# An attention and two-layer kernel on one core: planner latencies, due times, PSUM rings and two half-width chunks changed

## The chip, the cores and the metric

The kernel runs on one core of a Trainium2 chip. The metric is device time in microseconds (us) of one execution. Before the change the median of three runs is 897.53 us (896.87 to 906.74).

## The reference, cut to what matters

```python
def phi(x):                                   # x: (4, 8, 576, 64), omega: (128, 64)
    proj = einsum('bhsd,md->bhsm', x, omega)
    h = proj - sum(x * x, axis=-1, keepdims=True) / 2
    h = h - max(h, axis=-1, keepdims=True)
    return exp(h) / sqrt(m)
q_p, k_p = phi(q * D**-0.25), phi(k * D**-0.25)
kv, z = einsum('bhsm,bhsd->bhmd', k_p, v), sum(k_p, axis=2)
attn = einsum('bhsm,bhmd->bhsd', q_p, kv) / (einsum('bhsm,bhm->bhs', q_p, z)[..., None] + 1e-06)
x = attn.transpose(0, 2, 1, 3).reshape(2304, 512)
x = softplus(x @ w_in) @ w_out                # 512 -> 2048 -> 512
x = silu(x @ w_in2) @ w_out2                  # 512 -> 2048 -> 512, float32 out
```

The weights arrive as float64 bits and are turned into float32 on the chip.

## The kernel before, in words

Every large product is done on pairs of reduced-precision numbers: a float32 operand is split into a high part (a cast on ScalarE) and a low part (`diff`, a subtraction on VectorE), and three matmuls replace one. The program has four stages on TensorE, in this order.

**Attention with the first product of layer 1.** There are five token blocks: four of 512 tokens (one batch each) and one of 256 (the four tails). `attention(b)` works in pieces, each a half of the heads of 256 tokens. A piece of k is *projection* (16 matmuls into two PSUM tiles), *exponential* on ScalarE, and the *kv* product. A piece of q is projection and exponential, and then twice (e = 0, 1): *flip* (four transposes into `pq`), a copy `qt` by ScalarE, *num* (by the halves of the array, into `pn`), a division on VectorE (`den`, `xn`), and *back* (two transposes into `px`). When both backs are there, ScalarE writes the high part of x and VectorE the low part. The square term of phi enters in one of two ways. With the "fold", ScalarE squares the transposed input and 16 further matmuls by `neg_half` (L577) add it to the projection; VectorE then takes one maximum (L590). Without it, a second copy of the input lies in natural order, ScalarE squares that, and VectorE makes a row sum (`sums`, L548), the maximum (L592) and two small shifts (L600, L601). Before the change the k and q pieces of batch 0 and the k tail of batches 0 and 1 use the fold (`n < 2`, `bp == 0`, `sb == 0`). `first_layer(sb)` multiplies block sb by 16 chunks of 128 columns of w_in: 12 matmuls of up to 512 columns (L819 to L821), a copy to `g` (L825) and a store to DRAM (L829). The attention of block sb + 1 is woven between the chunks of block sb.

**Second product of layer 1**, **first product of layer 2**, **second product of layer 2.** These use seven block products in place of eight (the order 1, 5, 6, 2, 7, 3, 4). Their weights are prepared in pairs of row blocks by `sums_of`: a load `raw` (L353), a scaling by ScalarE (L358), three steps on VectorE (L362, L367, L372), then casts and sums, and stores to a DRAM buffer `ws` (L460), eight pairs for each of three matrices. Pairs of the first two matrices are prepared during the first stage, those of the last during layer 2's first product. `load_w` (L1070) brings sets of block weights back from `ws`. `load_b` (L863) brings back the stored activations `gate`, softplus runs on them (L867), `combine` and `split` (L874, L889, L279) make the operands `g`, and the products are L941 and L947. Layer 2's first product is L1191; between its products ScalarE copies PSUM banks away (`snap`, L1201) and VectorE adds to them (L1206).

**What sets the order.** `Order` (L88 to L260) collects items, each with an engine, a time that it occupies the engine, a lag until its result can be used, the tiles that it takes, and a due time. A list scheduler then simulates the four queues with these numbers and writes out, for every engine, one fixed sequence; of the items that could start it takes the one due first. On the chip each engine goes through its own sequence in order and waits by semaphores. The numbers of the planner have no effect on the chip other than by this sequence. Of these numbers the change touches among others: the lag of ScalarE, the transfer model (`RATE` bytes per us, `ARRIVE` us), the slack that a due time gets (`WAIT`, `AHEAD`), how far ahead weights are fetched (`FETCH`, `EARLIER`), and the due time of each weight pair (`PREP`). PSUM has two rings of four banks, `bank` and `y`; `PLACE` says which of them kv, flip, num and back use, and the projections of batch 0 use `y`.

Of the kernel before, what the change touches and what calls it, by code (L numbers as in the profile page):

```python
# [18 lines left out]
P = 128  # L19
T = 256  # L20
# [29 lines left out]
STAY = 5.39  # L50
GT, TURN = 0.18, 0.1
# [9 lines left out]
BACKLOG, SOON = 1.0, 6.6  # L61
EARLIER = 23.24
AHEAD, WAIT = 2.88, 2
RATE = 380e3
ARRIVE = 2.0
ISSUE = 0.5
BEGIN = 36.0
SHARE = (2.2, 1.3, 1.75, 0.45, 0.0)
PREP = tuple(140.0 + 11.1 * n for n in range(8)) + tuple(237.9 + 12.7 * n for n in range(8)) + tuple(542.0 + 14.0 * n for n in range(8))
# [6 lines left out]
def on_act(n, psum=False):  # L76
    return ((0.04 if psum else 0.10) + n / 1193, 0.15)
# [183 lines left out]
def attention_moe_moe_kernel(  # L261
# [79 lines left out]
    def unpack(layer, fc, io, raw_tag, into, tf, first, after, due=None):  # L341
# [34 lines left out]
        b = add("ACT", (0.575, 0.15), scale, [a], alloc=[tf] if opens else [], uses=[traw] + ([] if opens else [tf]))  # L376
# [116 lines left out]
    def inputs(s, name, xT, xN, vs, fold, held, after):  # L493
# [31 lines left out]
        for i, (v, shape) in enumerate(vs or ()):  # L525
# [3 lines left out]
            def load_v(i=i, v=v, shape=shape, opens=opens):  # L529
                if tw is None:  # L530
                    x = get("ld", [P, VW], F32, f"v_{name}_{i}")
                else:
                    if opens:
                        s["both"] = get("wb", [P, 2 * VW], F32, f"v_{name}")
                    x = s["all"][:, XW:] if tw is here else s["both"][:, i * VW : (i + 1) * VW]
# [22 lines left out]
    def features(s, name, simple, fold, ins, cols, sq_of, psums):  # L558
# [6 lines left out]
        tps = [new(psums) for _ in range(2)]  # L565
# [74 lines left out]

    def main_cols():
        return [0, P, T, T + P], lambda sq, j: sq.rearrange("p (c e j) -> p j e c", c=2, e=2)[:, j]
# [16 lines left out]
    def k_half(n, half, simple, psums, due, after):  # L659
# [3 lines left out]
        ins = inputs(s, name, kT[n, :, 2 * half : 2 * half + 2, :], kN[n, :, :, hs, :], [(v1[n, :, :, hs, :], (2, 4))], n < 2, simple, after)  # L663
        cols, sq_of = main_cols()
        exps, tphis = features(s, name, simple, n < 2, ins, cols, sq_of, psums)
        tk = new(PLACE["kv"])
# [19 lines left out]
    def k_tail(bp, simple, psums, due, after):  # L686
# [3 lines left out]
        ins = inputs(s, name, kT[NT, :, :, bp * P : (bp + 1) * P], kN[NT, :, bp], vs, bp == 0, simple, after)  # L690
        exps, tphis = features(s, name, simple, bp == 0, ins, [hp * P for hp in range(NHP)], lambda sq, j: sq.rearrange("p (u i j) -> p j u i", u=2, i=2)[:, j], psums)
        for u in range(2):
            for i in range(2):
                tk = new(PLACE["kv"])
# [16 lines left out]
    def q_half(n, half, simple, psums, due, after):  # L711
# [3 lines left out]
        ins = inputs(s, name, qT[n, :, 2 * half : 2 * half + 2, :], qN[n, :, :, 4 * half : 4 * half + 4, :], None, sb == 0, sb == 0, after)  # L715
        cols, sq_of = main_cols()
        exps, tphis = features(s, name, simple, sb == 0, ins, cols, sq_of, psums)
# [4 lines left out]
        tx = new(PLACE["back"])  # L722
        backs = []
        for e in range(2):
            tq, tn, tqs, td, txn = new(PLACE["flip"]), new(PLACE["num"]), new("b2"), new("den"), new("b2")
# [51 lines left out]
            backs.append(add("PE", 0.23, back, [o1] + backs, alloc=[] if e else [tx], uses=[txn] + ([tx] if e else [])))  # L777
# [19 lines left out]
        xready[sb].append(add("DVE", V5, low, [h1], due=due, uses=[tx, xtile[at]]))  # L797

    xfirst = {}

# [4 lines left out]
    def first_layer(sb):  # L805
        w = width[sb]
        tx = [xtile[sb, half] for half in range(2)]
        for fc in range(NFC):
            th, tg = new("y"), new("ld")
# [3 lines left out]
            def gemm(fc=fc, s=s, name=name):  # L813
                ph = s["h"] = get("y", [P, 2 * T], F32, f"h_{name}")
# [551 lines left out]
```

## Time and profile before

| what | value |
|---|---|
| median of the runs | 897.53 us |
| profiled execution | 902.26 us, of which its span is 900.1 us |
| mean granted clock of TensorE | 0.992 |
| TensorE (PE) busy | 866.2 us, 96% of the span |
| VectorE (DVE) busy | 679.2 us, 75% |
| ScalarE (ACT) busy | 539.3 us, 60% |
| DMA | 253.22 MB, mean 281 GB/s |

The profiled execution is one run with a profiler on, and lies 4.7 us above the median. Busy shares are means over the whole span; the stages differ.

### The profile page before, as it was taken

The numbers are of one execution on the slowest core, as the hardware profiler recorded it, in microseconds if no ns is written. First come the engines' busy times: TensorE is split into PE (matmuls) and PEld (weight loads), VectorE is DVE, ScalarE is ACT, GpSimd is POOL, SyncE is SP. The second block draws the span as 40 slices with busy tenths as digits, with TensorE's granted clock in tenths as the row PEclk, the third lists the DMA queues.
The fourth block names the chain that finished last, engine by engine and source line by source line (L and its number), as shares of the span: only waits on it lengthen the run. The fifth ranks groups of instructions, "written<-read, shape, count | busy, mean of one in ns | idle before, by whom it ended". The sixth has DMA issues, their size and how long they took to land.

```text
span 900.1 us, 17506 instructions
## 1 busy us (share of the span) xinstructions
PE 866.2 (96%) x6548; PEld 807.6 (90%) x6548; DVE 679.2 (75%) x1239; ACT 539.3 (60%) x1088; POOL 1.3 (0%) x8
## 2 busy tenths in 40 slices
PE   8899989999999998999999999999999899999996
PEld 7778778877777888999999999999999899999996
DVE  4888887988889575688789934796853889778972
ACT  6967676767766564587574535676854645533330
POOL 0000000000000000000000000000000000000000
PEclk9999999999999999999999999999999999999999
DMA  7656857799989999958996799996869996699422
GB/s 246 219 174 215 292 174 260 266 328 394 331 307 344 376 330 381 322 185 283 368 340 207 251 372 347 352 320 223 293 226 338 362 363 235 217 372 345 140 85 70
DMA packets 148812, 253.22 MB, mean 281 GB/s; under 512 B 10488, under 2 KB 81272, under 8 KB 148728
## 3 DMA queue, kind: packets, MB, share of 16 engines
q1 hardware_dynamic: 148584, 251.98, 80.9%
q8 instruction: 51, 0.84, 0.4%
q14 instruction: 33, 0.27, 0.1%
q10 hardware_dynamic: 144, 0.13, 0.0%
HBM read 151.40 MB, written 100.66 MB: 280 GB/s over the span
## 4 chain that ended last, share of the span: by engine, by line
PE 50%; DMA 23%; DVE 14%; ACT 7%; issue 4%; SPq 1%; ACTq 0%; DVEq 0%
DMA raw<-in_w 13%; PE X L947 11%; PE X L941 9%; PE Z L947 5%; PE Z L941 5%; PE X L1191 3%; PE Y L947 3%; PE Y L941 3%; PE h L819 3%; DMA b<-gate 2%; PE h L820 2%; PE h L821 2%; DMA ws<-st 2%; DMA gate<-s 2%; PE Z L1191 2%
## 5 line engine op out<-in xcount | busy, mean ns | idle before, releaser
L819 PE MATMUL h<-x,wt 128*128 128x512 f32 (+1 forms) x320 | 122.4, 382 | 1.2 <-ACT g L825 1.2
L821 PE MATMUL h<-x,wt 128*128 128x512 f32 (+1 forms) x320 | 118.4, 370 | 0.4 <-DVE wt L279 0.4
L820 PE MATMUL h<-x,wt 128*128 128x512 f32 (+1 forms) x320 | 118.0, 369 | 0.0
L1191 PE MATMUL X<-x_x,w 128*128 128x384 f32 x576 | 109.0, 340 | 5.3 <-ACT s L1201 4.1
L889 ACT CAST g<-b 128x768 fp32r<-128x768 f32 x96 | 78.8, 838 | 57.6 <-PE X L947 19.4
L1191 PEld LDWEIGHTS X<-x_x,w 128*128 128x128 f32 x576 | 101.1, 190 | 8.8 <-ACT s L1201 5.7
L947 PE MATMUL X<-w,g 128*128 128x256 f32 x864 | 107.1, 283 | 0.5 <-DVE g L279 0.5
L279 DVE TENSOR_TENSOR g<-b,g 128x768 fp32r<-128x768 f32 x96 | 89.4, 953 | 22.1 <-ACT g L889 21.7
L947 PEld LDWEIGHTS X<-w,g 128*128 128x128 f32 x864 | 105.1, 192 | 0.9 <-DVE g L279 0.7
L941 PE MATMUL X<-g,w 128*128 128x384 f32 x576 | 103.2, 334 | 0.2 <-DVE g L279 0.2
L941 PEld LDWEIGHTS X<-g,w 128*128 128x128 f32 x576 | 100.0, 188 | 0.5 <-DVE g L279 0.5
L889 ACT CAST g<-t 128x768 fp32r<-128x768 f32 x72 | 58.8, 833 | 55.9 <-DVE t L874 28.4
L279 DVE TENSOR_TENSOR g<-t,g 128x768 fp32r<-128x768 f32 x72 | 67.6, 954 | 27.8 <-ACT g L889 27.7
L362 DVE TENSOR_SCALAR raw<-raw 128x512 uint32<-128x512 uint32 x64 | 26.8, 426 | 60.4 <-DMA raw<-in_w 57.1
L819 PEld LDWEIGHTS h<-x,wt 128*128 128x128 f32 x320 | 60.3, 189 | 11.6 <-ACT g L825 1.4
L821 PEld LDWEIGHTS h<-x,wt 128*128 128x128 f32 x320 | 60.3, 188 | 11.6 <-DVE wt L279 1.1
L820 PEld LDWEIGHTS h<-x,wt 128*128 128x128 f32 x320 | 60.5, 189 | 8.9
L358 ACT ACTIVATE pair<-raw 128x512 f32<-128x512 f32 x48 | 32.9, 693 | 52.6 <-DMA raw<-in_w 52.1
L279 DVE TENSOR_TENSOR st<-pair,st 128x512 fp32r<-128x512 f32 x72 | 49.1, 687 | 20.2 <-ACT st L450 19.9
L825 ACT COPY g<-h 128x512 f32<-128x512 f32 (+1 forms) x80 | 45.0, 566 | 19.5 <-PE h L821 11.9
L941 PE MATMUL Z<-g,w 128*128 128x384 f32 x288 | 53.5, 342 | 2.8 <-DMA w<-ws 2.8
L450 ACT CAST st<-pair 128x512 fp32r<-128x512 f32 x72 | 44.8, 630 | 17.6 <-DMA ws<-st 5.6
(119 smaller groups left out, 1528.5 us busy)
## 6 DMA issues: line engine op xcount, KB each, us to landing
w<-ws SPq DMA_DIRECT2D x42, 1024.0 KB, 8.1
b<-gate SPq DMA_DIRECT2D x48, 768.0 KB, 7.3
raw<-in_w SPq DMA_DIRECT2D x64, 512.0 KB, 6.1
gate<-s SPq DMA_DIRECT2D x96, 192.0 KB, 4.6
gate<-g SPq DMA_DIRECT2D x64, 256.0 KB, 4.5
ws<-st SPq DMA_DIRECT2D x16, 1024.0 KB, 7.6
ws<-st SPq DMA_DIRECT2D x16, 768.0 KB, 5.5
ws<-st SPq DMA_DIRECT2D x24, 512.0 KB, 5.4
```

What stands on the lines that cost most here:

```text
L279: nc.vector.tensor_tensor(o, a, b, op=ALU.subtract)
L358: nc.scalar.activation(into(), hif, AF.Copy, scale=2.0**-112)
L362: nc.vector.tensor_scalar(lo, lo, 29, None, op0=ALU.logical_shift_right)
L450: nc.scalar.copy(st[:, :, 0], of())
L819: nc.tensor.matmul(ph[:, :w], wt[:, 0, cs], xt[:, 0, :w], start=(cc == 0), stop=False)
L820: nc.tensor.matmul(ph[:, :w], wt[:, 0, cs], xt[:, 1, :w], start=False, stop=False)
L821: nc.tensor.matmul(ph[:, :w], wt[:, 1, cs], xt[:, 0, :w], start=False, stop=(cc == NCC - 1))
L825: nc.scalar.copy(s["g"][:, :w], s["h"][:, :w])
L889: nc.scalar.copy(g[:, :, 0], s[src][:, 2 * r : 2 * r + 2])
L941: nc.tensor.matmul(o[:, :HW_], w[:, 2 * r + k, a, cs], g[:, k, h], start=one, stop=(k == 1 and a == 1), skip_group_check=True)
L947: nc.tensor.matmul(o[:, a * 256 : a * 256 + 256], g[:, k, h, ts], w[:, 2 * r + k, v], start=one, stop=(k == 1 and h == 1), skip_group_chec ...
L1191: nc.tensor.matmul(s[x][:, :HW_], w[:, a, cs], xop[p][:, cc, h], start=(opens and cc == 0 and a == 0 and h == 0), stop=(cc == 1 and a == 1 ...
```

## The change

It has five parts. (1) The planner's numbers are set anew: ScalarE's lag 0.15 to 0.20 becomes 0.37, and 0.55 for the `qt` copy; a transfer's time goes from 2.0 us + bytes/380e3 to 2.3 us + bytes/360e3; slack, fetch distances, and due times (24 single ones for the weight pairs) get other values. (2) The fold stays for the four k pieces of batch 0 alone; the k tail of batches 0 and 1 and the four q pieces of batch 0 go the way of the row sums. (3) Batch 0 gets its own table of PSUM rings, `FIRST`, and `PLACE` is set otherwise. (4) The first two chunks of block 0 are computed by halves of 256 tokens, each as soon as its tokens are there, into the ring `bank`. (5) The weight pairs from number 12 on (of 24; before, from 16) are stored in four pieces rather than two.

```diff
-A5, A2, AE, AL = (0.52, 0.17), (0.30, 0.15), (1.0, 0.2), (0.97, 0.17)
+A5, A2, AE, AL = (0.52, 0.37), (0.30, 0.37), (1.0, 0.37), (0.97, 0.37)
-EARLY = 0
-PLACE = {"kv": "bank", "flip": "y", "num": "bank", "back": "y"}
-LEAD, TRAIL, EVERY, WINDOW_OF, FETCH = 0.11, 2.4, 3.8, 37.88, 10.05
+EARLY = 4
+PLACE = {"kv": "y", "flip": "y", "num": "bank", "back": "bank"}
+FIRST = {"k": "by", "q": "yy", "kv": "b", "flip": "b", "num": "b", "back": "y"}
+FOLD = (True, False, False)
+HALVES = (2, 0, 0, 0, 0)
+LEAD, TRAIL, EVERY, WINDOW_OF, FETCH = 0.05, 2.58, 3.13, 19.89, 27.81
-EARLIER = 23.24
-AHEAD, WAIT = 2.88, 2
-RATE = 380e3
-ARRIVE = 2.0
+EARLIER = (23.19, 33.84)
+APART = 12
+AHEAD, WAIT = 2.84, 4.21
+RATE = 360e3
+ARRIVE = 2.3
-PREP = tuple(140.0 + 11.1 * n for n in range(8)) + tuple(237.9 + 12.7 * n for n in range(8)) + tuple(542.0 + 14.0 * n for n in range(8))
+PREP = (115.8, 127.0, 153.9, 143.7, 172.8, 184.0, 194.9, 221.1, 239.2, 242.1, 258.9, 272.1, 289.7, 303.4, 318.1, 331.2, 529.3, 539.2, 580.2, 588.1, 606.2, 621.4, 615.8, 640.3)
...
+        fold = sb == 0 and FOLD[2]
+        ins = inputs(s, name, qT[n, :, 2 * half : 2 * half + 2, :], qN[n, :, :, 4 * half : 4 * half + 4, :], None, fold, sb == 0, after)
...
-            f1 = add("PE", 0.45, flip, exps, alloc=[tq], uses=tphis, wait=0.0 if simple else WAIT)
-            c1 = add("ACT", on_act(512, True), copy, [f1], alloc=[tqs], uses=[tq])
+            f1 = add("PE", 0.41, flip, exps, alloc=[tq], uses=tphis, wait=0.0 if simple else WAIT)
+            c1 = add("ACT", (0.47, 0.55), copy, [f1], alloc=[tqs], uses=[tq])
...
+            if fc < HALVES[sb]:
+                ch = 12 * mm(T)
+                for part in range(2):
+                    g1 = add("PE", ch, lambda gemm=gemm, part=part: gemm(part), xpart[sb, part] + [wready[fc]], due=due1[0, sb, 0 if not part else HALVES[sb] // 2] + ch * (fc + 1), loose=True, alloc=[] if part else [th], uses=tx + [wtile[fc // 2]] + ([th] if part else []))
+                    halves[part].append(g1)
...
-        sums_of(m, k, PREP[n], n < 16)
+        sums_of(m, k, PREP[n], n < APART)
```

**What moves on TensorE, in the attention of block 1.** These rows stand in its last piece, q3_1 (`pq` flips, `pn` num, `px` back, `h` a chunk of the first layer). Before:

```order
L821 MATMUL h_0_14_1604<-x1_0_1_687,wt_7_1583 128x512
L730 MATMUL pq_q3_1_0_1640<-ident_82,phi_q3_1_0_1596 128x128
...
L730 MATMUL pq_q3_1_1_1649<-ident_82,phi_q3_1_1_1625 128x128
L285 MATMUL pn_q3_1_0_1660<-kv1_99,qt_q3_1_0_1654 64x65 x8
L285 MATMUL pn_q3_1_1_1672<-kv1_99,qt_q3_1_1_1658 64x65 x8
L573 MATMUL pp_k4_0_0_1687<-om_sb_87,x_k4_0_1231 128x128
```

And of the change:

```order
L777 MATMUL px_q3_0_1535<-ident_82,xn_q3_0_0_1501 128x128 x2
L743 MATMUL pq_q3_1_0_1538<-ident_82,phi_q3_1_0_1467 128x128
...
L743 MATMUL pq_q3_1_1_1549<-ident_82,phi_q3_1_1_1483 128x128
L847 MATMUL h_0_11_1557<-x1_0_0_616,wt_5_1416 128x512
...
L849 MATMUL h_0_11_1557<-x1_0_1_678,wt_5_1416 128x512
L289 MATMUL pn_q3_1_0_1581<-kv1_99,qt_q3_1_0_1571 64x65 x8
L289 MATMUL pn_q3_1_1_1594<-kv1_99,qt_q3_1_1_1574 64x65 x8
```

Before, both flips and both nums follow each other with nothing between the second flip and the nums. Now a whole chunk (12 matmuls) stands between flips and nums, and the nums come three chunks earlier. From block 1 on, every num now has other matmuls between itself and its flip.

**What moves on SyncE, at the end of the first stage.** SyncE issues the transfers in this order (`gate` stores of chunks, `w2` loads of layer 1's second weights, `ws` stores of pairs, `b` loads of activations). Before:

```order
L829 DMA gate0_74<-g_4_8_4378 128x256
L829 DMA gate0_74<-g_4_9_4396 128x256
L460 DMA ws10_80<-st_10_7_0_4315 128x4x512
L1070 DMA w2_0_0_5_4415<-ws01_79 128x4x512
L829 DMA gate0_74<-g_4_10_4417 128x256
L829 DMA gate0_74<-g_4_11_4435 128x256
L829 DMA gate0_74<-g_4_12_4454 128x256
L1070 DMA w2_0_0_6_4458<-ws01_79 128x4x512
```

And of the change:

```order
L857 DMA gate0_74<-g_4_2_4224 128x256
L1104 DMA w2_0_0_5_4250<-ws01_79 128x4x512
L464 DMA ws10_80<-st_10_5_0_4227 128x2x512
L464 DMA ws10_80<-st_10_5_6_4230 128x512
...
L1104 DMA w2_0_0_6_4345<-ws01_79 128x4x512
...
L1104 DMA w2_0_0_4_4548<-ws01_79 128x4x512
L897 DMA b00_0_0_1_4559<-gate0_74 128x4x384
...
L464 DMA ws10_80<-st_10_6_0_4612 128x2x512
```

The load of weight set 5 stood behind the store of chunk 9 and the last store of pair 7 of the matrix `ws10`; now it stands behind the store of chunk 2. Pairs 6 and 7 of `ws10` are stored only after the loads for the second product, so their preparation falls into that product.

## Rows read from the trace of the kernel before

**Rows 1.** Busy time by stage: window, length, engines' busy us, clock, DMA share, GB/s.

```profile
0.00:60.00 60.00, 53.41 (x710) 44.37 (x711) 42.60 (x101) 46.76 (x131) 1.31 (x8) 1.00 0.64 211
60.00:345.00 285.00, 274.58 (x2311) 229.81 (x2310) 233.00 (x562) 195.46 (x465) 0.00 (x0) 0.99 0.86 301
345.00:395.00 50.00, 47.01 (x261) 46.36 (x261) 29.71 (x32) 30.86 (x44) 0.00 (x0) 0.97 0.85 300
395.00:525.00 130.00, 130.00 (x752) 130.00 (x751) 114.43 (x150) 75.59 (x96) 0.00 (x0) 1.00 0.85 288
525.00:720.00 195.00, 189.25 (x1091) 185.32 (x1090) 124.41 (x238) 120.02 (x256) 0.00 (x0) 0.99 0.90 314
720.00:887.00 167.00, 167.00 (x1394) 167.00 (x1393) 132.80 (x156) 70.58 (x98) 0.00 (x0) 1.00 0.70 240
887.00:900.00 13.00, 4.98 (x42) 4.78 (x40) 2.22 (x4) 0.00 (x0) 0.00 (x0) 0.84 0.25 76
```

**Rows 2.** TensorE's waits, 60 to 345 us: releaser: total us, times, longest.

```profile
PE pn_q L285 <- ACT qt_q L734: 4.5, 3, 2.2
```

**Rows 3.** Timeline of TensorE, 105 to 119 us: start, length, instruction, count, [idle before].

```profile
104.98 1.16 PE L573 MATMUL pp_q<-om_sb,x_q 64*128 64x128 f32 x16
...
116.21 1.18 PE L285 MATMUL pn_q<-kv,qt_q 128*64 128x65 f32 x32 [1.69 <-ACT qt_q L734]
117.32 1.75 PE L573 MATMUL pp_k<-om_sb,x_k 64*128 64x128 f32 x16
```

**Rows 4.** Busy time by window (columns of rows 1): the stretches behind three stalls.

```profile
116.20:121.40 5.20, 5.19 (x66) 4.46 (x66) 4.22 (x14) 2.58 (x5) 0.00 (x0) 0.67 0.48 152
352.30:355.50 3.20, 3.16 (x12) 3.16 (x13) 0.88 (x1) 1.86 (x4) 0.00 (x0) 0.65 1.06 402
701.60:703.50 1.90, 1.89 (x6) 1.90 (x7) 1.90 (x5) 1.13 (x3) 0.00 (x0) 0.50 1.06 400
```

**Rows 5.** Timeline of TensorE, start of layer 1's second product.

```profile
345.17 4.33 PE L941 MATMUL X<-g,w 128*128 128x384 f32 x24
352.34 6.00 PE L941 MATMUL Z<-g,w 128*128 128x384 f32 x24 [2.84 <-DMA w<-ws]
```

**Rows 6.** The chain of waits between 340 and 353 us: start, length, what.

```profile
340.75 1.02 SPq L460
...
341.82 10.47 DMA w<-ws
```

**Rows 7.** All engines' waits, 525 to 720 us.

```profile
ACT pair L358 <- DMA raw<-in_w: 28.4, 14, 3.7
```

**Rows 8.** Timelines around 698 us, ScalarE and then TensorE.

```profile
698.04 0.68 ACT L358 ACTIVATE pair<-raw 128x512 f32<-128x512 f32 x1 [3.56 <-DMA raw<-in_w]
...
701.61 3.63 PE L1191 MATMUL X<-x_x,w 128*128 128x384 f32 x11 [2.48 <-ACT s L1201]
```

**Rows 9.** The raw loads of line 353, 525 to 720 us.

```profile
DMA to landing us min/median/max: 3.6/5.3/9.9
```

**Rows 10.** Timeline of TensorE, a folded projection of q and what follows it.

```profile
31.26 0.49 PE L573 MATMUL pp_q<-om_sb,x_q 64*128 64x128 f32 x4
...
33.24 0.44 PE L764 MATMUL px_q<-ident,xn_q 128*128 128x128 f32 x2
```

**Rows 11.** Groups by line and shape: count, busy us, mean ns, idle before.

```profile
L548 DVE TENSOR_REDUCE sqs_q<-x_q 128x8 f32<-128x512 f32 x14 | 9.5, 680 | 0.9 <-ACT x_q L544 0.9
L600 DVE SCALAR_TENSOR_TENSOR mn_q<-sqs_q,mn_q 128x4 f32<-128x4 f32 x28 | 4.3, 154 | 0.0
L372 DVE SCALAR_TENSOR_TENSOR pair<-raw,pair 128x512 uint32<-128x512 uint32 x48 | 32.5, 687 | 0.5
L473 DVE TENSOR_TENSOR pair<-pair 128x256 f32<-128x256 f32 x96 | 40.3, 420 | 1.2
L825 ACT COPY g<-h 128x256 f32<-128x256 f32 x16 | 5.8, 375 | 6.6 <-DMA gate<-g 6.6
```

**Rows 12.** The page's DMA issues: stores of weight pairs, KB each, us to landing.

```profile
ws<-st SPq DMA_DIRECT2D x16, 1024.0 KB, 7.6
```

More of the change, by code (lines that the diff above doesn't have):

```diff
@@ L564, in features @@
         adds = []
-        tps = [new(psums) for _ in range(2)]
+        tps = [new(lane) for lane in psums]
         def project():
@@ L639, in features, with project_in, lane_of @@
         return [x for x, _ in res], [t for _, t in res]
+    def project_in(use, psums):
+        return psums[use] if isinstance(psums, dict) else (psums, psums)
+    def lane_of(use, psums):
+        return psums[use] if isinstance(psums, dict) else PLACE[use]
     def main_cols():
@@ L662, in k_half @@
         hs = slice(4 * half, 4 * half + 4)
-        ins = inputs(s, name, kT[n, :, 2 * half : 2 * half + 2, :], kN[n, :, :, hs, :], [(v1[n, :, :, hs, :], (2, 4))], n < 2, simple, after)
+        fold = n < 2 and FOLD[0]
+        ins = inputs(s, name, kT[n, :, 2 * half : 2 * half + 2, :], kN[n, :, :, hs, :], [(v1[n, :, :, hs, :], (2, 4))], fold, simple, after)
         cols, sq_of = main_cols()
-        exps, tphis = features(s, name, simple, n < 2, ins, cols, sq_of, psums)
-        tk = new(PLACE["kv"])
+        exps, tphis = features(s, name, simple, fold, ins, cols, sq_of, project_in("k", psums))
+        tk = new(lane_of("kv", psums))
         b, h0 = n // 2, 4 * half
@@ L721, in q_half @@
             xready[sb] = xready.get(sb, [])
-        tx = new(PLACE["back"])
+        tx = new(lane_of("back", psums))
         backs = []
         for e in range(2):
-            tq, tn, tqs, td, txn = new(PLACE["flip"]), new(PLACE["num"]), new("b2"), new("den"), new("b2")
+            tq, tn, tqs, td, txn = new(lane_of("flip", psums)), new(lane_of("num", psums)), new("b2"), new("den"), new("b2")
             def flip(e=e, tq=tq):
@@ L807, in first_layer, with gemm @@
         tx = [xtile[sb, half] for half in range(2)]
+        halves = [[], []]
+        before = last[0]
         for fc in range(NFC):
-            th, tg = new("y"), new("ld")
+            if fc and fc == HALVES[sb]:
+                prev = before
+                for i in halves[0] + halves[1]:
+                    od.items[i]["behind"] = prev
+                    prev = i
+                last[0] = prev
+            lane = "bank" if fc < HALVES[sb] else "y"
+            th, tg = new(lane), new("ld")
             s = {}
             name = f"{sb}_{fc}"
-            def gemm(fc=fc, s=s, name=name):
-                ph = s["h"] = get("y", [P, 2 * T], F32, f"h_{name}")
+            def gemm(part=None, fc=fc, s=s, name=name, lane=lane):
+                opens = "h" not in s
+                if opens:
+                    s["h"] = get(lane, [P, 2 * T], F32, f"h_{name}")
+                ts = slice(0, w) if part is None else slice(part * T, (part + 1) * T)
+                ph = s["h"][:, ts]
                 wt = wts[fc // 2][:, fc % 2]
@@ L1070, in load_w @@
                     nc.sync.dma_start(w.bitcast(F32).rearrange("p k h w -> p k (h w)"), ws[wm][q * KQ : (q + 1) * KQ, ROW[p]].rearrange("k p w -> p k w"))
-                wload[p] = add("SP", (ISSUE, 0), load_w, [i for k in range(q * KQ, (q + 1) * KQ) for i in kept[wm, k]], alloc=[tws[p]], nbytes=P * KQ * 2048, turn=t0, after=t0 + n * each - EARLIER)
+                wload[p] = add("SP", (ISSUE, 0), load_w, [i for k in range(q * KQ, (q + 1) * KQ) for i in kept[wm, k]], alloc=[tws[p]], nbytes=P * KQ * 2048, turn=t0, after=t0 + n * each - EARLIER[layer])
             for sc in range(SC):
@@ L1287, in attention @@
                 f(n, half, simple, psums, due, after)
-    attention(0, "y")
+    attention(0, {use: ["y" if c == "y" else "bank" for c in lanes] if len(lanes) > 1 else "y" if lanes == "y" else "bank" for use, lanes in FIRST.items()})
     for fc in range(NFC):
```

41 lines of the change are left out of this document (22 added, 19 removed).

## The prediction

> **What bounds the kernel now.** I read the busy time by stage first. TensorE works 274.6 of the 285 us between 60 and 345 us, 47.0 of 50 around the start of layer 1's second product, all 130 us of its remainder, 189.3 of 195 in layer 2's first product and all 167 us of the last product before its tail [rows 1]. So TensorE is the bound everywhere, and only three things can move the time: work that TensorE no longer does, its idle time, which is 10.4 us, 3.0 us and 5.7 us in the three stages that have any after the first 60 us, and the slow stretch behind an idle time. That last one is in the windows behind three stalls: the granted clock there is 0.67, 0.65 and 0.50 as a mean over 5.2, 3.2 and 1.9 us, that is, part of each at the lower level, 1.2 GHz [rows 4].
>
> Then I read, stage by stage, which wait ends last. In the attention it is the num product behind ScalarE's copy `qt`, 4.5 us in three waits [rows 2]; one such place has 1.69 us of idle time, and the 16 projections behind it take 1.75 us where the same 16 took 1.16 us shortly before [rows 3]. At the second product TensorE has done the first set of 24 matmuls in 4.33 us, waits 2.84 us for the load of weight set 5, and the next 24 take 6.00 us [rows 5]. The chain of waits shows why: SyncE's queue stood in the store of a weight pair (L460) until the load was issued at 341.82 us, and it landed 10.47 us later [rows 6]. In layer 2's first product ScalarE sits 3.56 us before a scaling (L358) whose raw weights have not landed, the PSUM copy queued behind it is late, and TensorE idles 2.48 us [rows 8]. Over that stage ScalarE waits 28.4 us for such raw loads [rows 7], which mostly costs nothing, since TensorE idles 5.7 us in all.
>
> **The change, part by part.** The sum is made against the profiled execution, 902.3 us, which is 4.7 us above the median of the runs; the same 4.7 us come off at the end.
>
> *Fold removed in five pieces* (four q and one k tail). From the first folded projection to the next instruction of another kind 1.98 us pass [rows 10]; an unfolded projection takes 1.16 us [rows 3]. Five times 0.82 us is **-4.1 us** of TensorE's own work in a stretch where it is busy 53.4 of 60 us [rows 1]. If VectorE or the loads now hold TensorE there, nothing of it comes off: bounds -4.1 and 0. I take -4.1, as TensorE's busy share there is 89%.
>
> *What the fold's removal adds.* ScalarE's five squares stay as they are. VectorE gets five row sums of 0.680 us and twenty shifts; with 0.154 us for each, the twin of L600 counted like it, that is 3.4 + 3.1 = 6.5 us [rows 11]. VectorE has 17 us free in the first 60 us, but of the following 285 us it is busy 233.0, 82%, with the operands of each next token block at the end of its queue [rows 1]. Below nothing it can't go, above it is the whole 6.5 us. I take **+3 us**, the middle: the additions fall in the emptier first stretch, and what they push goes into the fuller second. Five more input loads of 256 KB are 1.3 MB, 6.2 us at the 211 GB/s of that stretch; the DMA share there is 0.64, so 21 of the 60 us are free [rows 1]. Bounds 0 and +6.2; I take 0, as the natural copies are needed late (first by the shift behind the maximum).
>
> *Chunks by halves, rings.* Two chunks become 48 matmuls of 256 columns from 24 of 512: the same columns, so 0. From above, 24 more instructions cost no more each than a whole matmul of a projection, 1.16/16 = 0.07 us [rows 3], so +1.7 us; from below, -2 us, if they fill waits of the first stage. The ring tables have no row before; the waits they could change are the 6.6 us in which TensorE is not busy in the first 60 us, of which a good part is the start itself [rows 1]. I take 0 with bounds of -3 and +3.
>
> *Flips and nums drawn apart.* A num needs its flip, ScalarE's copy and the wake-up between. The order now puts a chunk between them where nothing stood. I take all 4.5 us of these waits [rows 2], and the lost clock behind one of them, 5.2 us x (1 - 0.67) = 1.7 us [rows 4]: **-6.2 us**. The stage's other 5.9 us of idle time, short waits on divisions, exponentials and first-layer copies [rows 1], I leave. Bounds: -12.1 us if everything goes, 0 if each wait comes back at another place, which the piece of VectorE's work above could bring about.
>
> *Second product's start.* Weight set 5 is issued seven chunks of block 4 earlier, and no longer behind pair 7's stores. 2.84 us of idle time and 6.00 - 4.33 = 1.67 us at the lower clock go [rows 5]: **-4.5 us**. Bound from the other side: 0, if the next sets or the first operands are then late. On SyncE the `b` loads of the second unit now stand ahead of the partial stores, which takes a wait out of their way; I cost that at nothing, because TensorE is busy throughout 395 to 525 us [rows 1].
>
> *Raw loads of the last matrix.* They are due earlier, singly. The one late load that costs most is worth 2.48 us and the slow stretch behind it: 11 of these matmuls, at 4.33/24 = 0.18 us each 2.0 us, took 3.63 us, so 1.6 us [rows 5, 8]. Bounds: -7.3 us (all 5.7 us of idle time and the 1.6) and 0. I take half of the costliest one, **-2 us**, since loads issued earlier meet transfers that already fill 0.90 of the DMA's time [rows 1]. What decides is how long a raw load of 512 KB takes from issue to landing. The row says 3.6 us at the least and 5.3 us at the median [rows 9]; the planner reckoned with 2.0 + 524288/380e3 = 3.4 us and now with 2.3 + 524288/360e3 = 3.8 us, so the new setting is nearer and still short.
> The Trainium skill (DMA: Bandwidth & Descriptors, section Anatomy of one DMA — SWDGE (gpsimd) path) gives a fit of about 2.0 us plus bytes/436e3, which is an estimated 3.2 us for this load; the page made the fit on another issuing path. By that rule the old setting would have been long enough, earlier loads would buy nothing, this term would be 0 and the sum 886 rather than 884; the trace's 5.3 us disagrees with it, and the row decides.
>
> *The last product and the tail* are left as they are: no idle time in 167 us, and the 13 us behind it are stores [rows 1].
>
> Sum: -4.1 + 3 - 6.2 - 4.5 - 2 = -13.8 us. 902.3 - 13.8 = 888.5 us as a profiled execution, less 4.7: **884 us**.
>
> **The rivals.** *VectorE becomes the bound in blocks 0 and 1.* Its added 6.5 us come through whole, and the waits that leave the nums come back at the first chunk of block 1 or 2, for the low half of x: the terms +3 and -6.2 become +6.5 and 0, the sum -4.1 and the time 893 us; with half of this, 889 us. For it speaks VectorE's 82% in that stage; against it, that a fifth of the stage is still free. Chance 0.20.
>
> *All stalls go.* The bounds -12.1 and -7.3 hold, VectorE's term is 0: -4.1 - 12.1 - 4.5 - 7.3 = -28.0, 869.5 us. For it: each stall is a matter of order, not of capacity. Against it: the raw loads share a DMA that is 0.90 busy. With a good part of it, 870 to 878 us; chance 0.17.
>
> *The change does not do what it says*: the order is apart but new waits of the same size appear at other places, and only the folds are won: 893 to 900 us. Chance 0.10.
>
> *Slower than before: SyncE's queue blocks.* The loads of weight sets, 1 MB each, now stand among the stores of block 4's chunks. If one has to wait for its buffer, which a weight pair's store must have left, every chunk store behind it waits too, ScalarE runs out of tiles for its copies and TensorE stops. That coupling exists: before the change ScalarE already idled 6.6 us for chunk stores before these 16 copies [rows 11]. Five tiles of 256 columns are about five chunks of 12 x 0.12 = 1.4 us (0.12 estimated as two thirds of the 0.18 us for 384 columns), so it decides from a wait of some 7 us on. A pair's store of 1 MB takes 7.6 us to land [rows 12]; with three loads waiting that long, 23 us come on top: 907 us. A lesser variant is pairs 6 and 7 of `ws10`, now prepared within the second product: seven steps of 0.687 us and seven of 0.420 us each, 15.5 us of VectorE's time for both [rows 11], where it has 15.6 us free of 130 [rows 1]. Against the first: the later pairs no longer use the buffers that the loads use. Chance 0.05.
>
> The forecast itself, 878 to 889 us, has 0.48.
>
> **How the numbers follow.** The range of 870 to 895 us leaves out part of the last two rivals and of the all-stalls case, 2 in 10 together. Two per cent, about what a measurement of this kernel can tell from no change, is 18 us: faster means below 879.6 us, slower above 915.5 us. Below 879.6 us lie the all-stalls case and a fifth of the forecast: 0.26. Above 915.5 us lies only the blocked queue at a higher price: 0.03. The rest, 0.71, is within.
>
> **What would show it.** Folds: no `neg_half` rows for q, and TensorE's busy time 4 us less in the first stage. Flips: no wait of num on `qt` over 0.3 us after 60 us, and the 60 to 345 us stage with some 6 us of idle time. Second product: 24 matmuls on set 5 in 4.3 us with no wait for `w<-ws`. Raw loads: fewer and shorter TensorE waits on `snap` copies. VectorE as the bound shows as a wait of the first chunk of block 1 or 2 on the low half of x. The prediction is wrong if such a wait exceeds 6 us, if the second product idles after all for an operand `g`, or if the stage from 525 us on gets longer.

## The result

The changed kernel takes **869.4 us** (median of 4 runs, 868.7 to 870.3) against 897.2 us for the kernel before in the same job, a ratio of 0.967 (95% interval 0.960 to 0.973). The forecast was 884 us, range 870 to 895. The direction was right; the forecast fall of 13.5 us is half of the measured 27.8 us, and the time lies just under the range. It is also the time of the rival "all stalls go" (869.5 us), to which the prediction gave a chance of 0.17; that the two agree to 0.1 us is in part luck, as shown below.

The profiled execution has a span of 867.4 us, 32.7 us shorter than the one before. Of these, 4.7 us are the distance at which the profiled run of before stood above its median. In this job the kernel before spread from 896.8 to 906.7 us in four runs, over all jobs from 893.4 to 906.7 us; the changed kernel's four runs lie within 1.6 us. The times by stage below are of one profiled execution of each kernel.

### The profile page after: what moved, and what is told of

Read it like the earlier page. It is cut to its first block, busy times and chain, and to the rows that moved or that the text cites. A ratio compares the mean times of both kernels' runs of the same rounds, so it can differ in the third digit from the quotient of the medians.

```text
span 867.4 us, 17421 instructions
## 1 busy us (share of the span) xinstructions
PE 851.2 (98%) x6492; PEld 799.8 (92%) x6492; DVE 682.3 (79%) x1264; ACT 546.2 (63%) x1088; POOL 1.3 (0%) x8
## 4 chain that ended last, share of the span: by engine, by line
PE 84%; DMA 8%; DVE 4%; ACT 2%; issue 1%; SPq 1%; ACTq 0%; DVEq 0%
PE X L981 12%; PE X L1225 12%; PE X L975 12%; PE Z L981 6%; PE Z L975 6%; PE Z L1225 6%; PE h L847 5%; PE h L849 5%; PE h L848 5%; PE Y L981 3%; PE Y L1225 3%; PE Y L975 3%; DMA ws<-st 3%; DMA raw<-in_w 2%; PE pp_q L577 2%; PE pn_q L289 2%
## 5 line engine op out<-in xcount | busy, mean ns | idle before, releaser
L847 PE MATMUL h<-x,wt 128*128 128x512 f32 (+1 forms) x328 | 124.1, 378 | 0.1
L849 PE MATMUL h<-x,wt 128*128 128x512 f32 (+1 forms) x328 | 119.6, 365 | 0.0
L848 PE MATMUL h<-x,wt 128*128 128x512 f32 (+1 forms) x328 | 119.6, 364 | 0.0
L1225 PE MATMUL X<-x_x,w 128*128 128x384 f32 x576 | 106.0, 334 | 0.0
L847 PEld LDWEIGHTS h<-x,wt 128*128 128x128 f32 x328 | 61.8, 189 | 11.3 <-ACT g L853 0.3
L849 PEld LDWEIGHTS h<-x,wt 128*128 128x128 f32 x328 | 61.9, 189 | 10.3
L283 DVE TENSOR_TENSOR st<-pair,st 128x512 fp32r<-128x512 f32 x72 | 48.7, 686 | 28.4 <-ACT st L454 28.3
L848 PEld LDWEIGHTS h<-x,wt 128*128 128x128 f32 x328 | 62.0, 189 | 8.6
L981 PE MATMUL Z<-w,g 128*128 128x256 f32 x432 | 53.8, 283 | 0.0
L1225 PE MATMUL Z<-x_x,w 128*128 128x384 f32 x288 | 53.8, 334 | 0.0
L981 PEld LDWEIGHTS Z<-w,g 128*128 128x128 f32 x432 | 52.7, 192 | 0.0
```

Source lines behind the costliest of these rows:

```text
L283: nc.vector.tensor_tensor(o, a, b, op=ALU.subtract)
L847: nc.tensor.matmul(ph, wt[:, 0, cs], xt[:, 0, ts], start=(opens and cc == 0), stop=False, skip_group_check=part is not None)
L848: nc.tensor.matmul(ph, wt[:, 0, cs], xt[:, 1, ts], start=False, stop=False, skip_group_check=part is not None)
L849: nc.tensor.matmul(ph, wt[:, 1, cs], xt[:, 0, ts], start=False, stop=(cc == NCC - 1), skip_group_check=part is not None)
L981: nc.tensor.matmul(o[:, a * 256 : a * 256 + 256], g[:, k, h, ts], w[:, 2 * r + k, v], start=one, stop=(k == 1 and h == 1), skip_group_chec ...
L1225: nc.tensor.matmul(s[x][:, :HW_], w[:, a, cs], xop[p][:, cc, h], start=(opens and cc == 0 and a == 0 and h == 0), stop=(cc == 1 and a == 1 ...
```

## The profile after

The stages of the changed kernel by busy time (columns as in [rows 1]), without the last product; each window is cut at the first matmul of a stage:

```profile
0.00:45.50 45.50, 38.31 (x563) 31.56 (x563) 33.32 (x96) 37.61 (x110) 1.31 (x8) 1.00 0.72 246
45.50:328.20 282.70, 281.60 (x2404) 237.44 (x2403) 235.10 (x566) 201.90 (x477) 0.00 (x0) 1.00 0.88 304
328.20:503.00 174.80, 174.80 (x1011) 174.80 (x1010) 154.29 (x207) 111.38 (x148) 0.00 (x0) 1.00 0.91 316
503.00:678.00 175.00, 175.00 (x1011) 174.73 (x1009) 110.07 (x218) 115.52 (x240) 0.00 (x0) 1.00 0.89 316
```

TensorE idles 1.1 us between 45.5 and 328 us and not at all in the two stages behind it, and the granted clock is 1.00 in each of these rows. Its waits after 60 us are two, where the kernel before had 10.4 us of them up to 345 us alone:

```profile
PE pkv_kt L712 <- DMA v_kt<-in_vt: 0.8, 1, 0.8
PE pp_q L577 <- DVE mn_k L604: 0.2, 1, 0.2
```

The place of [rows 3] in TensorE's timeline now reads so (start, length, instruction):

```profile
96.15 0.60 PE L743 MATMUL pq_q<-ident,phi_q 128*128 128x128 f32 x4
...
99.45 1.15 PE L289 MATMUL pn_q<-kv,qt_q 128*64 128x65 f32 x32
```

The chunk's 12 matmuls lie between flip and num, and no idle time is marked. And the start of the second product, against [rows 5]:

```profile
328.22 4.33 PE L975 MATMUL X<-g,w 128*128 128x384 f32 x24
332.39 4.32 PE L975 MATMUL Z<-g,w 128*128 128x384 f32 x24
336.55 4.32 PE L975 MATMUL X<-g,w 128*128 128x384 f32 x24
```

Three sets at full pace, no wait for `w<-ws`. In layer 2's first product ScalarE's waits for raw loads, 28.4 us in [rows 7], are down to this row (503 to 678 us):

```profile
ACT pair L362 <- DMA raw<-in_w: 2.7, 5, 0.7
```

The stages, from first matmul to first matmul, with TensorE's idle time in parentheses; "first" is the time up to the first chunk, "blocks" from there to the second product, and "last" ends with the start of the last matmul. The idle time is the sum of the gaps between TensorE's records in the trace:

```
                          first       blocks        2nd product  1st, layer 2  last         runs: median, ratio
before                    52.3 (4.7)  292.9 (10.4)  179.8 (3.0)  184.4 (5.3)  182.3 (0.5)
changed                   45.5 (5.3)  282.8  (1.1)  174.7 (0.0)  174.9 (0.0)  181.3 (0.0)  869.4  0.967
place_back                46.4 (5.3)  284.6  (2.4)  174.7 (0.0)  175.2 (0.2)  185.1 (3.3)  876.5  0.975
lag_back                  48.7 (6.4)  283.5  (2.4)  174.7 (0.0)  175.1 (0.1)  181.8 (0.3)  874.5  0.972
prep3_back                46.4 (4.2)  282.4  (0.8)  174.7 (0.0)  175.7 (0.4)  188.5 (4.6)  877.9  0.975
wire_back                 45.3 (5.2)  284.3  (2.5)  180.7 (3.3)  180.8 (3.5)  185.4 (2.1)  883.8  0.982
slack_back                49.3 (5.3)  281.9  (1.4)  175.6 (0.5)  175.2 (0.2)  185.4 (3.6)  878.3  0.977
apart16                   46.3 (4.3)  290.9  (6.6)  179.4 (2.8)  174.7 (0.0)  186.3 (3.0)  887.5  0.985
halves0                   51.4 (7.0)  278.7  (0.9)  175.0 (0.0)  177.5 (1.7)  182.4 (0.4)  874.4  0.971
fold_on_halves0           54.4 (5.1)  277.7  (0.0)  174.7 (0.0)  177.2 (1.6)  183.2 (1.4)  877.0  0.973
after_rawlag1             45.5 (3.9)  281.9  (0.1)  174.7 (0.0)  176.3 (1.3)  182.6 (0.6)  870.9  0.970
structure_old_numbers     54.3 (7.0)  295.8 (10.4)  177.0 (1.7)  183.5 (5.2)  182.4 (0.5)  902.8  1.002
attention_numbers_only    51.1 (5.4)  287.0  (5.7)  183.6 (5.5)  180.4 (3.4)  185.4 (2.7)  894.7  0.994
loads_numbers_only        52.0 (7.2)  287.7  (7.6)  175.2 (0.2)  179.2 (2.8)  183.7 (2.0)  890.2  0.990
before_rawlag3            51.9 (4.0)  293.7  (9.5)  180.7 (3.7)  180.2 (2.9)  186.4 (4.1)  902.9  1.003
before_lag_wait_place     64.5(14.1)  286.6  (5.5)  181.4 (4.1)  185.2 (6.3)  186.2 (2.6)  911.0  1.012
before_nofold             54.6 (7.9)  296.6 (12.1)  179.6 (4.1)  186.1 (8.0)  182.3 (0.5)  910.0  1.011
before_apart12            53.4 (4.8)  290.2  (8.9)  177.0 (1.3)  184.7 (6.1)  182.4 (0.6)  896.9  0.996
```

Ratios are to the kernel before in the same job (its medians there 897.2 to 900.3 us); their intervals reach 0.003 to 0.007 to each side. The changed kernel was timed in the first job alone. A difference to its 869.4 us is therefore one between jobs, and one of 3 us or less says nothing.

## The experiments

**One part of the change taken back.** General ring table as before:

```diff
-PLACE = {"kv": "y", "flip": "y", "num": "bank", "back": "bank"}
+PLACE = {"kv": "bank", "flip": "y", "num": "bank", "back": "y"}
```

> The changed kernel with the old general ring table alone (kv and num in bank, flip and back in y), the batch 0 table kept. In its order five num products of blocks 1 to 4 stand within 0.8 us of TensorE's work behind their flip, where the changed kernel has none under 3.2 us. Theory 1 (the rings, not ScalarE's lag in the planner, draw flips and nums apart): waits of num on the qt copy come back, 1.0 to 2.0 us each with a slow stretch behind, so 5 to 9 us more than 869.4 us: 874 to 879 us, all of it before the second product. Rival (the lag and the slack do it): within 2 us of 869.4 us.

Total as theory 1 said, reason not. Flips and nums stand together again, yet all waits of num on `qt` after 60 us are this row:

```profile
PE pn_q L759 <- ACT qt_q L747: 0.6, 1, 0.6
```

So a short distance in the order costs little by itself; what ScalarE has in its queue ahead of the copy matters too, as a run below shows at one place. The blocks lost 1.8 us, and 3.8 us were lost at the far end, at the start of the last product.

ScalarE's lags back to 0.15 to 0.20:

```diff
-A5, A2, AE, AL = (0.52, 0.37), (0.30, 0.37), (1.0, 0.37), (0.97, 0.37)
+A5, A2, AE, AL = (0.52, 0.17), (0.30, 0.15), (1.0, 0.2), (0.97, 0.17)
...
```

(The lines that are left out set the lag of the other copies, of the scaling and of `qt` back in the same way.)

> The changed kernel with ScalarE's old lags in the planner (0.15 to 0.20, the qt copy like any other). In its order the smallest distance of a num from its flip in blocks 1 to 4 is 1.6 us. Theory 1 (rings): no wait of num on qt over 0.3 us, total within 3 us of 869.4 us. Rival (the lag is what removes the stalls, in the attention and at the PSUM copies of layer 2's first product): 6 to 12 us slower, 875 to 881 us.

Between the two: 5 us, of which 3.2 before the first chunk, which neither theory named. After 60 us no num waits for `qt`.

Due times of the last matrix's pairs (n from 16) back to 542 + 14 n:

> The changed kernel with the old due times of the last matrix's eight pairs (542 to 640 us, 14 us apart). Theory 2 (the due times of these pairs took the waits out of layer 2's first product): ScalarE's waits for raw loads stop PSUM copies again and that stage takes 4 to 9 us more than its 175.0 us, total 873 to 878 us. Rival (the transfer model and the lags did it, single due times do not matter): total within 2 us of 869.4 us.

The total is as expected, the place is wrong: layer 2's first product kept 175.7 us, and the last product lost 7 us. There TensorE waits for operands (670 to 760 us):

```profile
PE Z L981 <- DVE g L283: 1.3, 1, 1.3
PE X L981 <- DVE g L283: 1.3, 1, 1.3
PE Y L981 <- ACT g L923: 1.2, 1, 1.2
```

At the first two of these waits, VectorE's queue has steps of the late pairs' preparation among the splits of `g`; before the third it has stood 3.39 us until a load of activations landed:

```profile
680.74 0.42 DVE L477 TENSOR_TENSOR pair<-pair 128x256 f32<-128x256 f32 x1
681.08 0.95 DVE L283 TENSOR_TENSOR g<-b,g 128x768 fp32r<-128x768 f32 x1
681.94 0.42 DVE L477 TENSOR_TENSOR pair<-pair 128x256 f32<-128x256 f32 x1
...
695.48 1.76 DVE L908 TENSOR_TENSOR t<-t,b 128x1536 f32<-128x1536 f32 x1 [3.39 <-DMA b<-gate]
```

The changed kernel has such steps there too, but later, from 693 us on. Which of the two costs more was not tested.

The transfer model back:

```diff
-RATE = 360e3
-ARRIVE = 2.3
+RATE = 380e3
+ARRIVE = 2.0
```

> The changed kernel with the old transfer model in the planner (2.0 us + bytes/380e3). Theory 2 (due times): within 2 us of 869.4 us, no TensorE wait over 1 us in layer 2's first product. Rival (the longer transfer time is what brings the raw loads early enough): 4 to 9 us more in that stage, total 873 to 878 us. Since all loads of the program are planned by this model, waits on loads could also appear in the attention, 1 to 3 us.

The longer transfer time is worth 14 us in this set, the most of any planner number tried, and in all three products. ScalarE's waits for raw loads in layer 2's first product rose to 13.8 us (503 to 690 us):

```profile
ACT pair L362 <- DMA raw<-in_w: 13.8, 12, 2.4
```

The Trainium skill (DMA: Bandwidth & Descriptors, section Anatomy of one DMA — SWDGE (gpsimd) path) puts such a load at an estimated 3.2 us by its fit of 2.0 us plus bytes/436e3. By that rule going back to 3.4 us would have been free. In wire_back the raw loads of this stage took 3.7 to 11.0 us from issue to landing, 4.7 at the median, and in the changed kernel 3.7 to 9.1 us, 5.1 at the median. So the trace disagrees for these loads, which SyncE issues, and the measurement decides. The 14 us are not the price of this one error alone, since the model plans every transfer of the program.

Stores of pairs 12 to 15 in two pieces again (`APART = 16`):

> The changed kernel with the old way of storing for weight pairs 12 to 15 (two stores of larger tiles, in the ring of the weight sets). In its order 6.7 us more of VectorE's work stands ahead of the second product. Theory 4 (VectorE in blocks 1 to 4 is what the moved pairs relieve): 3 to 7 us more before the second product starts, 872 to 877 us. Rival (VectorE never ends a wait there): within 2 us of 869.4 us before the second product; its first weight sets might wait for buffers, up to 3 us.

18 us, far over both: 8.1 in the blocks, 4.7 in the second product, 5.0 in the last one. In the blocks TensorE idles 5.4 us at one place for a chunk's copy. The chain of waits there (start, length, what):

```profile
317.52 0.07 ACT g L853
317.59 11.55 DMA gate<-g
...
329.86 0.36 ACT g L853
...
330.27 0.58 PE h L847
```

In this chain 11.55 us pass from a chunk's copy to the landing of its store, at 329.14 us. But the copy starts only 0.7 us later, and ScalarE's timeline shows why:

```profile
322.80 0.35 ACT L853 COPY g<-h 128x256 f32<-128x256 f32 x1
324.34 1.57 ACT L923 CAST g<-t 128x768 fp32r<-128x768 f32 x2 [1.19 <-DVE t L908]
326.49 0.67 ACT L362 ACTIVATE pair<-raw 128x512 f32<-128x512 f32 x1 [0.59 <-DMA raw<-in_w]
328.47 1.48 ACT L901 ACTIVATE b<-b 128x1536 f32<-128x1536 f32 x1 [1.31 <-DMA b<-gate]
329.86 0.63 ACT L853 COPY g<-h 128x256 f32<-128x256 f32 x2
```

Casts, a scaling and a softplus stand between the two copies in ScalarE's order, and each of them waits first, two of them for loads. The store landed at 329.14 us and the softplus was done at 329.95 us, so either would have held the copy back. The prediction's slower rival, a weight-set load that waits for its buffer and blocks SyncE's queue for some 7 us, is not what shows: before such loads SyncE waits at most 1.1 us at a time here. Where the 9.7 us of the two layers' second products come from stays open.

Two chunks whole again (`HALVES = (0, 0, 0, 0, 0)`), and the same with the fold on again (`FOLD = (True, True, True)`):

> The changed kernel without the halving of the first two chunks. TensorE then starts the first layer later, with the fold's place still saved. Theory 5 (all due times are fitted to the structure): 3 to 8 us slower, mostly before the second product. Rival (the two halves cost and bring nothing, as the prediction took it): within 2 us of 869.4 us.

> The changed kernel without halved chunks and with the fold back on the k tail and the four q pieces. To be held against halves0: 80 matmuls more, 5.5 us by the rows of both traces, 6.5 us less on VectorE, and natural inputs of q not loaded. If TensorE's work counts whole: 5 to 6 us more than halves0, in the first 50 us. If the late natural inputs and row sums cost as much as the matmuls saved (kernel before_nofold lost by the removal): within 2 us of halves0 or less.

By the medians the halves are worth 5 us, not 0. The first chunk starts 5.9 us earlier, but 4.1 us of that are given back in the blocks, so that 1.8 us are left at the second product; 2.6 us more lie in layer 2's first product, which has no halves. By the ratios it is 3.7 us, and their intervals overlap, so how much the halves bring stays open. The fold's removal is worth 2.6 us by the medians (877.0 to 874.4), where the four runs of each overlap; its matmuls take 6.2 us in this trace and shorten "first" by 3.0 us.

**One part of the change alone.** Planned time of raw loads 3 us longer, in the kernel before:

```diff
-                it["end"] = wire + ARRIVE
+                it["end"] = wire + ARRIVE + it["lag"]
...
-        a = add("SP", (ISSUE, 0), load, alloc=[traw], nbytes=P * DM * 8, after=after, due=due)
+        a = add("SP", (ISSUE, 3.0 if layer or io else 0), load, alloc=[traw], nbytes=P * DM * 8, after=after, due=due)
```

> The kernel before, with one number changed in the planner: the raw loads of the weight pairs are planned to take 3 us longer than the model says; due times, rings, fold, lags, all other transfers as before. The flips and nums of blocks 1 to 4 still stand next to each other. Theory 3 (what held TensorE in the attention and in layer 2's first product alike was ScalarE's queue, waiting in order for raw loads planned too short): ScalarE's waits for raw loads between 60 and 720 us fall from 57 us to under 20 us, TensorE's idle time from 60 to 345 us from 10.4 to under 5 us, the first product of layer 2 from 184.4 to 176 to 179 us; in all 10 to 16 us under the kernel before. Rival (theory 1, rings; and flips next to nums): the attention keeps its idle time, only layer 2's first product gains, 4 to 6 us.

Theory 3 falls. ScalarE's waits for raw loads of pairs between 60 and 720 us went from 52.1 us to 0.2, and the attention kept its idle time. The wait of [rows 3] is still there; ScalarE's and TensorE's timelines show what holds the copy:

```profile
113.02 0.65 ACT L825 COPY g<-h 128x512 f32<-128x512 f32 x1
113.49 0.75 ACT L358 ACTIVATE pair<-raw 128x512 f32<-128x512 f32 x1
114.06 0.66 ACT L825 COPY g<-h 128x512 f32<-128x512 f32 x1
...
114.53 1.17 ACT L734 COPY qt_q<-pq_q 128x512 f32<-128x512 f32 x2
...
115.26 0.94 PE L285 MATMUL pn_q<-kv,qt_q 128*64 128x65 f32 x24 [1.67 <-ACT qt_q L734]
```

Two chunk copies and a scaling stand in the order between the flip and its copy, with no load late. Layer 2's first product gained 4.2 us, as the rival said, but the last product lost 4.1 us, and by the medians the kernel is 3.5 us slower, which neither range had.

Lags, slack and general ring table in the kernel before:

```diff
-A5, A2, AE, AL = (0.52, 0.17), (0.30, 0.15), (1.0, 0.2), (0.97, 0.17)
+A5, A2, AE, AL = (0.52, 0.37), (0.30, 0.37), (1.0, 0.37), (0.97, 0.37)
...
-PLACE = {"kv": "bank", "flip": "y", "num": "bank", "back": "y"}
+PLACE = {"kv": "y", "flip": "y", "num": "bank", "back": "bank"}
...
-AHEAD, WAIT = 2.88, 2
+AHEAD, WAIT = 2.84, 4.21
...
```

> The kernel before, with ScalarE's lags, the slack and the general ring table of the change; transfer model, due times, fold and the rest as before. In its order no num of blocks 1 to 4 stands within 1.7 us of its flip (the kernel before has eight within 1 us). Theory 1 (what the prediction reckoned with): no waits of num on qt after 60 us, 6 us or more gained before the second product, 888 to 893 us. Theory 3 (ScalarE's queue held by raw loads): ScalarE still waits over 40 us for raw loads, other waits take the place of those of num, less than 4 us gained in the attention and none in layer 2's first product: 893 to 899 us.

The blocks gained 6.3 us, as the prediction had reckoned for the flips drawn apart. But batch 0 took 12.2 us longer, and the total is over both ranges. The longest of batch 0's new waits is again one for a copy (5 to 65 us):

```profile
PE pn_q L285 <- ACT qt_q L734: 4.6, 3, 3.8
PE pp_k L573 <- ACT phi_k L617: 3.3, 2, 3.0
```

The table `FIRST` is missing here; that it would have saved these 12.2 us was not tested.

The fold taken off in the kernel before (`n < 2` kept for k; False for the tail and q):

> The kernel before, with the fold taken from the k tail and the four q pieces of batch 0 and nothing else changed. 80 matmuls of TensorE go, 5.5 us by the rows of both traces (144 fold matmuls took 9.9 us), VectorE gets 6.5 us. If TensorE's own work counts whole: 891 to 893 us. Rival (VectorE's additions come through as later operands): 896 to 900 us, with a wait of a first chunk on the low half of x.

Slower by 1.1%, over both ranges, although TensorE has 5.9 us less to do. Batch 0's nums now wait for copies (5 to 60 us):

```profile
PE pn_q L285 <- ACT qt_q L734: 3.7, 2, 1.9
```

Pairs from 12 on stored in pieces, in the kernel before (`n < 12`):

> The kernel before with only the way of storing pairs changed (from pair 12 on in four pieces). Theory 4 (the stores of the last pairs of the middle matrix and the loads of the second product's weight sets share a ring and SyncE's queue, as kernel apart16 showed with 5.4 us at the chunk copies): the wait for weight set 5 at the second product's start goes, 3 to 8 us less, 889 to 896 us. Rival (it matters only within the fitted set): 896 to 905 us, the wait back at another set.

The wait for weight set 5 went and the second product gained 2.8 us; the total fell by 3.3 us. What was worth 18 us in the fitted set is worth 1 to 6 us here (ratio 0.993 to 0.999).

**Numbers against structure.** All numbers of before in the changed structure without halves:

> The changed kernel with all of the planner's numbers of before (lags, transfer model, slack, fetch distances, due times), keeping its rings, its fold for k of batch 0 alone and its way of storing pairs; the two chunks are not halved. To be held against halves0, which differs from it in the numbers alone. Theory 5 (the numbers, fitted as one set to this structure, carry the gain; single parts are worth nothing alone): 890 to 905 us. Rival (the structure carries it, above all the stores of pairs in smaller pieces): 872 to 882 us.

Theory 5 holds: 902.8 us with the old numbers, 874.4 us with the new ones (halves0), and the changed structure with the old numbers is no faster than the kernel before (ratio 1.002). The other corner, the new numbers in the whole old structure, was not run. Split in two groups:

> The changed kernel without halved chunks and with the old numbers for the weights (transfer model, issue windows, fetch distances, all pair due times), the numbers for the attention new (ScalarE's lags, slack, due times of pieces and chunks). Theory 5a (the stage up to the second product is made by the attention's numbers, the stages behind it by the weights' numbers): up to the second product within 4 us of halves0 (330 us), layer 2's first product 180 to 184 us; total 882 to 890 us. Rival 5b (raw loads in ScalarE's queue hold the attention too, so that the weights' numbers are needed there): up to the second product over 338 us, total 890 to 900 us.

> The counterpart: the numbers for the weights new, those for the attention old, chunks not halved. Theory 5a: up to the second product 342 to 350 us, as with all numbers old (350), the stages behind it near their floor (175, 176, 182): total 886 to 894 us. Rival 5b: up to the second product under 338 us, total 876 to 884 us.

Up to the second product ("first" and "blocks") the four corners are 350.1 (both old), 338.1 (attention's new), 339.7 (loads' new), 330.1 us (both new): -12.0 and -10.4 alone, -20.0 together. There both 5a and 5b are half right. By the medians it is -8.1, -12.6 and -28.4 us: with the attention's numbers alone the second product loses 6.6 us and the last one 3.0. Single traces carry this split, one 2.7 us above its median and one 2.5 us below, so a few us of it are not certain.

The old slack alone in the changed kernel (`AHEAD, WAIT = 2.88, 2`, `STAY = 5.39`, `GT = 0.18`), and a raw load 1 us longer:

> The changed kernel with only the old slack before flips and projections (2 us rather than 4.2), tile-change cost and stay bonus. In its order two nums stand 0.9 us behind their flip, others 1.5. Theory 5a: waits of num on qt and of flips on exponentials come back, 3 to 7 us more up to the second product, 872 to 877 us. Rival (the distance between flip and num does not matter as long as ScalarE's queue is not held by raw loads, as in place_back): within 2 us of 869.4 us.

> The changed kernel with the raw loads of weight pairs planned to take 1 us longer than the new transfer model says. ScalarE's waits for raw loads fall from 12 us to under 6 us. Theory 5 (waits of ScalarE as such cost nothing; what counts is whether they reach TensorE, whose idle time is at its floor behind 45 us): 868 to 874 us, no faster. Rival (each us less of ScalarE's waiting is worth something): 863 to 867 us, faster than both kernels.

slack_back lost 9 us: 3.8 before the first chunk, none in the blocks, 4.1 in the last product. after_rawlag1 brought ScalarE's waits for raw loads from 11.8 us to 2.9 us over the whole run and gained nothing.

**Versions that might have been faster.** A raw load 1 us longer for the first two matrices alone, and `HALVES = (3, 0, 0, 0, 0)`:

> The changed kernel, with the raw loads of the first two matrices' pairs planned 1 us longer and those of the last matrix as in the change. If the stage gains of after_rawlag1 stay and its 1.3 us wait in layer 2's first product goes: 867 to 868.5 us. If every new number moves waits at random by a microsecond or two: 868 to 873 us.

> The changed kernel with three halved chunks rather than two. If the halves fill TensorE's waits at the end of batch 0's attention, where the changed kernel still idles 3.6 us before three backs: 866 to 869 us. If two halves already fill what can be filled, and the other numbers are fitted to two: 870 to 875 us.

870.7 us (ratio 0.967, 0.964 to 0.970) and 873.7 us (0.972, 0.968 to 0.975): neither beats the changed kernel.

## Why the prediction was wrong

By stage, the forecast was -7.3 us up to the second product, -4.5 in it, -2 in layer 2's first product and 0 in the last. The two traces differ by -17.0, -5.1, -9.5 and -1.0 us. Two steps failed: up to the second product the sum left most of TensorE's idle time standing and added 3 us for VectorE, and in layer 2's first product it took half of one wait where all of them went.

*Fold, -4.1 us: too small for the matmuls, and wrong on what they are worth.* The fold rows fell from 144 to 64 and from 9.9 to 4.0 us of TensorE's time, so 5.9 us, 1.2 for each piece where the prediction had 0.82. The term also counted them as time on the path by itself. Removed alone, the time rises by 1.1%.

*VectorE, +3 us: wrong.* Up to the second product VectorE worked 275.6 us before [rows 1] and 268.4 us now, the sum of the first two windows above. The prediction named the move of pairs 6 and 7 of `ws10` into the second product, 15.5 us, but only as a danger there; it did not take those 15.5 us out of the stage to which it added 6.5. VectorE still has 20 us free in the second product, and after 60 us TensorE waits 0.2 us for VectorE in all.

*Flips and nums, -6.2 us: the failed step is "The stage's other 5.9 us of idle time ... I leave".* The blocks' idle time went from 10.4 to 1.1 us. Of the 17.0 us up to the second product, 8.7 are idle time (0.6 us more in "first", 9.3 less in the blocks), 5.9 the fold and 1.7 the lost clock of [rows 4]; 0.7 us are left over. The reason given for the wait, distance in the order, was also incomplete: place_back has the short distances and hardly the wait, and at the place of [rows 3] before_rawlag3 shows the copy held by what ScalarE has queued ahead of it.

*Second product, -4.5 us: right.* It measured -5.1 us.

*Raw loads, -2 us: the second failed step is "I take half of the costliest one".* The stage fell by 9.5 us, more than the bound of -7.3. 1008 matmuls at 4.16/24 us are 174.7 us; the 184.4 us of before, less that and less 5.3 us of idle time, leave 4.4 us. The matmuls behind the 2.48 us wait make 1.6 of these, as the prediction had it. The other 2.8 us, which it left out, lie at ten waits, the clock at 1.00 at nine of them, so:

```profile
562.48 1.20 PE L1191 MATMUL X<-x_x,w 128*128 128x384 f32 x6
564.24 1.31 PE L1191 MATMUL X<-x_x,w 128*128 128x384 f32 x6 [0.55 <-ACT s L1201]
565.39 2.24 PE L1191 MATMUL Z<-x_x,w 128*128 128x384 f32 x12
```

From 562.48 to 565.39 us 12 matmuls take 2.91 us, where 2.08 are the full pace: 0.55 us idle and 0.28 us more. Nor were the raw loads all of it. before_rawlag3, where ScalarE hardly waits for them, gains 4.2 us in this stage, and its two waits left are for VectorE (1.5 and 0.8 us). What brings the other 5.3 us was not tested by itself.

*The last product, 0: -1.0 us. The 4.7 us off at the end* did not carry over: the changed kernel's profiled run (869.2 us) lies on its median. They made the forecast look nearer than its terms were, and the all-stalls rival exact: its terms sum to -28.0 us where the profiled executions differ by 33.0, and the 4.7 us fill the gap.

*Above all, the sum of terms.* Taken back one at a time from the changed kernel, lags, rings, last due times, transfer model, slack, stores and halves cost 5, 7, 8.5, 14, 9, 18 and 5 us, 67 us together where all is worth 28. Added alone to the kernel before, the parts tried gave +10.6, +11.5 and -3.3 us of median (before_nofold, before_lag_wait_place, before_apart12, each against before in its job). The gain belongs to the set: no engine but TensorE was over 88% busy in any stage [rows 1], and the changed kernel shows that an order almost without waits was there to be found; with the old numbers the same structure has 10.4 us of idle time in the blocks, as the kernel before. That was the rival's argument, "each stall is a matter of order, not of capacity", and it deserved more than 0.17.

The single costs are not prices of what each number means. halves3 takes nothing back and is still 4.3 us slower than the changed kernel (after_rawlag1 and rawlag1_not_last 1.5 and 1.3, which lies within what jobs differ by). So a part of each cost may be what any other order would have cost. What stays open is which single number does most of it in the first stage; in the traces the two groups share it about equally.

## What to carry to other kernels

Where a planner writes the order, weigh a change of all its numbers against the floor of the bound engine (matmuls times their full-clock step, plus head and tail), and ask whether any other engine stands in the way of it; pricing single waits finds only part. A part of such a set says little alone: one that brings 18 us in the set brought almost nothing outside it. A short wait of TensorE costs more than its idle time, here 0.28 us more at full clock and 1.6 us more where the clock fell behind it. Count what waits cost from rows, as the stage's length less matmuls times step.

## What the runs showed that I had not expected

A change of planner numbers in one stage was often paid for far behind it: old due times for the last matrix cost 7 us in the last product and 0.8 us in their own stage; old slack in the attention cost 4 us in the last product, 350 us and more behind it. And the kernel with fewer waits spread less: in the same job, four runs each, the kernel before ranged over 10 us and the changed one over 1.6 us. That the waits make the spread is not shown.
